# Cosine attention and highway FFN on one core: batch 0 by query tiles, k on seven-token lanes, batch 0's norms by Ln and Exp

## The chip, the core and the metric

The kernel runs on one core of a Trainium2 chip. The core has five instruction queues: PE (TensorE, matmuls and their weight loads), DVE (VectorE), ACT (ScalarE), POOL (GpSimd) and SP (SyncE, which here only issues DMAs). The time is the device time of one execution in microseconds; less is better. Inputs and output lie in HBM, the on-chip memories are SBUF (128 lanes, here also called partitions) and PSUM (eight banks of 128 x 512 fp32), into which PE writes.

## What is computed

q, k and v are 8 batches x 12 heads x 448 tokens x 64 fp32. Rows of q and k are divided by their norms, so the scores are cosines over tau = 0.1. After a softmax over keys and the product with v, the heads of a token stand side by side (768 wide) and go through a highway layer.

```python
q_n = q / (np.linalg.norm(q, axis=-1, keepdims=True) + 1e-06)
k_n = k / (np.linalg.norm(k, axis=-1, keepdims=True) + 1e-06)
attn = softmax(q_n @ k_n.T / tau)          # per batch and head
x = (attn @ v) as [8 * 448, 12 * 64]
H = np.maximum(x @ w_h, 0.0)
T = sigmoid(x @ w_t + b_t)
out = T * H + (1.0 - T) * x
```

Since the cosines are at most 1, the kernel leaves out the subtraction of the maximum: exp(10) is harmless. It computes in fp16 with fp32 sums.

## The kernel before

**Layout.** The 12 heads of a batch make 6 pairs (head p and p + 6) and 3 groups of 2 pairs. q is loaded so that a lane holds seven neighbouring tokens ("seven-token lanes": 64 lanes for the even heads, 64 for the odd ones, 1792 contiguous bytes each). k and v are loaded otherwise: 384 tokens as 128 lanes of three tokens, and the last 64 tokens by a DMA of their own (`kt`, `vt`). q comes by SP's queue as fp32; k and v by POOL's queue, which casts to fp16 on the way. For batch 0 alone k comes as fp32 in six pieces by ACT's and SP's queues, into the output buffers `os` (`ld_k0`).

**Stages of a batch.** Squares on ACT (L368, L388 and L391, tails L402), sums of squares on DVE (L376, L397, L404), the inverse root on DVE by a bit trick and two Newton steps, seven small instructions (`newton`, L416 to L423; four times for batch 0, on parts), scaling to fp16 on POOL (q L434, k L495, tails of k L502; a few on DVE in batch 0), transposes on PE through PSUM (q L446, k L460 and L465) and copies back to SBUF on DVE (L451, L471; in pieces L473, L475 for batch 0).

For each pair then: six score matmuls of 448 queries, in twos that use the two halves of the array (`scores`, L531), one for the tail keys of both heads (L542), seven exps of 448 columns on ACT (L537, L544), and `attend`: per 128 queries one product with the tail of v (L556) and six with v (L561), for the last queries eight half-wide ones (L569). The column of ones in `vp` gives the sum of the softmax; DVE takes its reciprocal (L576) and evicts the product into `x` (L577). `vp` is filled by copies on DVE (L509) and, for the tail, casts on POOL (L519).

`ffn` works on 128 tokens at a time, three such tiles and a half one per batch: transposes of x on PE (L600), a copy (L602), products with w_t and then w_h (L616, in the half tile L613), the bias on DVE (L625), tanh on ACT (L632; the sigmoid is 0.5 tanh(z/2) + 0.5), gate arithmetic on DVE (L628, L634, L637), the last addition on POOL (L642; at the end DVE), the store on SP (L652, L649). All four tiles of a batch read `x` as one piece, so none starts before all six pairs of that batch are attended.

**Order.** Nothing is scheduled by the compiler. All operations of all batches are made as a list (`op`, class `Plan`), with the tiles they read and write. `ORDER` is a permutation of that list, written out as numbers, and `SLOTS` says which buffer of each ring every tile takes. Each engine executes its operations in this order, one after the other. So batches overlap as ORDER has it: loads, norms and transposes of later batches stand between scores of one and FFN tiles of another. The main loop also adds waits of its own ("port"): a POOL operation of certain kinds waits for the DVE operation of such a kind that stands before it. Before any real work PE executes 18 matmuls on zeros (L279).

Of the kernel before, what the change touches and what calls it, by code (L numbers as in the profile page):

```python
# [8 lines left out]
FP32 = mybir.dt.float32  # L9
# [120 lines left out]
}  # L130


PORT = ("nt", "gt", "gg", "vc", "qn", "kn", "kb", "vt", "out")


class Op:
# [65 lines left out]
def kernel(  # L202
# [11 lines left out]
    nc = tc.nc  # L214
# [555 lines left out]
```

## Time and profile before

| what | us |
|---|---|
| median of 3 runs | 271.3 (270.35 to 271.45) |
| the profiled execution | 270.06 |
| its span, first to last instruction | 268.3 |
| PE busy | 251.6 |
| DVE busy | 233.4 |
| ACT busy | 214.5 |
| POOL busy | 169.8 |
| mean granted PE clock | 0.958 of full |

The span is the time between the first and the last instruction in the profile; the execution's own time is somewhat longer. A matmul's end is modelled, so a PE that is busy throughout is not thereby at its best. In the rows that follow, L12 is line 12 of the kernel, "B" are PSUM banks, and "<-" in a wait names what ended it.

### The profile page before, as it was taken

To read this page: it belongs to the slowest core of one execution; us is meant where nothing else is said; L and a number is where in the kernel's file an instruction comes from. 1 tells how busy PE (TensorE), PEld (TensorE's weight loads), DVE (VectorE), ACT (ScalarE), POOL (GpSimd) and SP (SyncE) were. 2 spreads that over 40 slices of the span, in tenths; PEclk is the share of its full clock that TensorE was granted. 3 is DMA by queue.
4 is the path that set the end of the run, shared out by engine and by line. 5 is a ranking of instruction groups with operands and counts; after the bars stand their busy time and mean duration, and the time that the engine had idled before them with its cause. 6 is when DMAs were issued, how large, how long until landed. Compare 5 with 4: busy or idle time off the path is not lost.

```text
span 268.3 us, 7687 instructions
## 1 busy us (share of the span) xinstructions
PE 251.6 (94%) x3042; PEld 158.8 (59%) x3042; DVE 233.4 (87%) x523; ACT 214.5 (80%) x421; POOL 169.8 (63%) x212
## 2 busy tenths in 40 slices
PE   8375999999999999999999999999999999999990
PEld 2122566656756576657656685666666675667660
DVE  2987988799999999999989899999998788657993
ACT  3389899999589997999899996999979757883120
POOL 6467878306975679668957397659555686320650
PEclk9755799999999999999999999999999999999998
DMA  7999999999307990496995972990513101052146
GB/s 173 298 290 181 208 270 261 213 255 126 44 18 221 234 182 14 146 257 159 151 142 185 164 107 67 330 135 4 147 23 100 29 15 49 0 147 65 29 135 190
DMA packets 51092, 38.64 MB, mean 144 GB/s; under 512 B 37488, under 2 KB 47856, under 8 KB 51056
## 3 DMA queue, kind: packets, MB, share of 16 engines
q1 hardware_dynamic: 25888, 26.75, 36.2%
q0 software_dynamic: 24896, 11.21, 33.1%
q8 instruction: 24, 0.39, 0.5%
q10 hardware_dynamic: 272, 0.20, 0.2%
q14 instruction: 12, 0.10, 0.1%
HBM read 38.34 MB, written 11.01 MB: 184 GB/s over the span
## 4 chain that ended last, share of the span: by engine, by line
PE 81%; DMA 6%; DVE 4%; ACT 4%; SPq 1%; issue 1%; POOL 1%; ACTq 0%; DVEq 0%
PE B L616 33%; PE B L531 12%; PE B L561 10%; PE B L613 5%; DMA os<-in_k_dram 4%; PE B L556 4%; PE B L600 4%; PE B L446 3%; PE B L542 3%; PE B L569 3%; PE B L460 3%; ACT E L537 3%; DMA out_dram<-os 1%; PE B L465 1%; DVE hm L628 1%
## 5 line engine op out<-in xcount | busy, mean ns | idle before, releaser
L537 ACT ACTIVATE E<-B 128x448 f16<-128x448 f32 x288 | 137.4, 577 | 15.6 <-PE B L531 12.6
L642 POOL TENSOR_TENSOR os<-x,hm 128x384 f32<-128x384 f16 x53 | 47.5, 911 | 50.2 <-DVE hm L637 39.6
L616 PEld LDWEIGHTS <-xT 128*128 128x128 f16 x576 | 51.2, 98 | 34.8 <-issue 7.5
L434 POOL TENSOR_TENSOR qn<-qr,y 128x448 f16<-128x448 f32 x47 | 43.4, 934 | 24.6 <-issue 8.1
L616 PE MATMUL B<-wh,xT 128*128 128x384 f16 x288 | 57.6, 326 | 0.0
L616 PE MATMUL B<-wt,xT 128*128 128x384 f16 x288 | 56.7, 326 | 0.0
L531 PE MATMUL B<-qT,kT 64*128 64x448 f16 x288 | 43.5, 367 | 2.8 <-DVE kT L473 1.5
L561 PE MATMUL B<-vp,E 128*128 128x65 f16 x864 | 44.5, 195 | 0.0
L561 PEld LDWEIGHTS <-E 128*128 128x128 f16 x864 | 39.1, 99 | 2.9
L632 ACT ACTIVATE tt<-z 128x768 f16<-128x768 f32 (+1 forms) x32 | 25.3, 793 | 18.5 <-DVE z L625 14.8
L495 POOL TENSOR_TENSOR kp<-kr,y 128x384 f16<-128x384 f16 x42 | 34.3, 827 | 8.2 <-DVE tt L634 2.6
L628 DVE SCALAR_TENSOR_TENSOR hm<-B,x 128x384 f16<-128x384 f32 x56 | 30.5, 549 | 3.0 <-PE B L616 1.7
L556 PE MATMUL B<-vp,Et 128*128 128x130 f16 x144 | 32.3, 224 | 0.0
L625 DVE TENSOR_TENSOR z<-B,bias 128x384 f32<-128x384 f32 x48 | 25.9, 551 | 6.5 <-PE B L616 5.5
L544 ACT ACTIVATE Et<-B 128x448 f16<-128x448 f32 x48 | 27.9, 597 | 3.1 <-PE B L542 2.8
L577 DVE SCALAR_TENSOR_TENSOR x<-B,rd 128x448 f16<-128x448 f32 x48 | 29.2, 617 | 0.6
L376 DVE TENSOR_REDUCE n<-sq 128x14 f32<-128x896 f32 (+1 forms) x25 | 25.8, 1040 | 1.2 <-ACT sq L368 1.2
L397 DVE TENSOR_REDUCE n<-sq 128x18 f32<-128x1152 f32 (+2 forms) x17 | 21.5, 1269 | 4.2 <-ACT sq L388 3.8
L368 ACT ACTIVATE sq<-qr 128x896 f32<-128x896 f32 (+1 forms) x24 | 23.1, 978 | 1.1 <-DMA qr<-in_q_dram 1.1
L531 PEld LDWEIGHTS <-kT 64*128 64x128 f16 x288 | 10.3, 94 | 20.1 <-issue 12.3
L556 PEld LDWEIGHTS <-Et 128*128 128x128 f16 x144 | 14.1, 98 | 7.9 <-issue 4.7
L542 PE MATMUL B<-qT,kT 128*128 128x448 f16 x48 | 17.4, 371 | 1.1 <-DVE kT L475 1.1
(59 smaller groups left out, 363.3 us busy)
## 6 DMA issues: line engine op xcount, KB each, us to landing
qr<-in_q_dram SPq DMA_DIRECT2D x7, 1344.0 KB, 7.6
out_dram<-os SPq DMA_DIRECT2D x48, 192.0 KB, 3.3
kr<-in_k_dram POOLq DMA_DIRECT2D x7, 576.0 KB, 12.2
vr<-in_v_dram POOLq DMA_DIRECT2D x7, 576.0 KB, 10.3
kt<-in_k_dram SPq DMA_DIRECT2D x16, 96.0 KB, 6.4
vt<-in_v_dram SPq DMA_DIRECT2D x16, 96.0 KB, 7.5
out_dram<-os SPq DMA_DIRECT2D x16, 96.0 KB, 2.9
qr<-in_q_dram SPq DMA_DIRECT2D x3, 448.0 KB, 6.9
```

Of the source, the lines that this page charges most:

```text
L434: ENG[eng].tensor_mul(R("qn", 3 * b + g)[:, :, t, :], R("qr", b)[:, g + 3 * t, :].rearrange("l (j d) -> l j d", d=D), R("y", b)[:, c : c + ...
L495: ENG[eng].tensor_mul(R("kp", 6 * b + p).rearrange("l c t d -> l t c d"), a, kcol(b, p))
L531: nc.tensor.matmul(R("B", ("S", n, c, t))[:, 0:S], lhsT=R("kT", i)[ln, s, 128 * c : 128 * c + 128], rhs=R("qT", i)[ln, s, :], start=True, ...
L537: nc.scalar.activation(R("E", n)[:, at : at + 7, :].rearrange("l j x -> l (j x)"), R("B", ("S", n, c, t))[:, 0:S], AF.Exp)
L544: op("ACT", f"expt {n}", lambda: nc.scalar.activation(R("Et", n).rearrange("l j x -> l (j x)"), R("B", ("St", n))[:, 0:S], AF.Exp), r=[("B ...
L556: nc.tensor.matmul(U[:, 2 * c : 2 * c + 2, :], lhsT=Et[:, 2 * c : 2 * c + 2, :].rearrange("l j x -> l (j x)"), rhs=vp[:, 6:8, 0:65], start ...
L561: nc.tensor.matmul(U[:, 2 * c + t, :], lhsT=E[:, at : at + 2, :].rearrange("l j x -> l (j x)"), rhs=vp[:, 3 * t + m, 0:65], start=False, s ...
L577: op("DVE", f"ev {n}", lambda: nc.vector.scalar_tensor_tensor(out=R("x", b)[:, :, D * p : D * p + D], in0=U_()[:, :, 0:D], scalar=0.0, in1 ...
L616: nc.tensor.matmul(P[:, 0:MH], lhsT=xT[:, cc, :], rhs=w_[:, cc, MH * mh : MH * mh + MH], start=(cc == 0), stop=(cc == CC - 1))
L625: op("DVE", f"za {g} {mh}", lambda at=at, sl=sl: nc.vector.tensor_add(R("z", g)[:, sl], R("B", at)[:, 0:MH], biast[:, :] if tail else bias ...
L628: op("DVE", f"hm {g} {mh}", lambda at=at, sl=sl, mh=mh: nc.vector.scalar_tensor_tensor(out=R("hm", g)[:, sl], in0=R("B", at)[:, 0:MH], sca ...
L642: op(eng, f"out {g} {mh}", lambda sl=sl, mh=mh: ENG[eng].tensor_add(R("os", g)[:, sl], xpart(mh), R("hm", g)[:, sl]), r=[("gg", g), ("x", ...
```

## The change

**k like q.** k is loaded on seven-token lanes by one DMA per batch (three for batch 0, one per group), always on POOL's queue with the cast. One function now does each stage for q and k: `ld_qk`, `norm`, `scale`, `turn`. A group of k takes seven transposes instead of eight; the DMA for the tail, its square, its sum, its two multiplies (L502) and the buffers `kt`, `kb`, `kp` are gone. The last 64 keys of both heads of a pair still need a block-diagonal tile for the tail scores, so the copy to SBUF is now one of 2 x 384 columns and two of 64 lanes x 2 x 64 columns (`cpt`), into buffers whose other halves were set to zero at the start. v follows the same assignment of tokens: it comes by two DMAs of 64 lanes, its tail is each lane's seventh token.

**Batch 0 by query tiles.** `attend0` takes a group and a tile of 128 queries (the fourth: 64), with scores of 128 (64) columns, exps of 512 and 384 columns, and its own eviction. The FFN's tiles of batch 0 read only the matching part of x, so `ffn(0, i)` can stand as soon as the three groups are attended for tile i. Group 0's turned q and k lie in a spare slot of the ring `x`.

**Norms of batch 0.** y = exp(-0.5 ln(n2 + 1e-14)) by two ACT operations per group in place of Newton. Ln is in another table set of ACT than tanh, so set 6 is loaded at the start and set 0 after the third of these (`table2`).

**Order and rings.** `ORDER` and `SLOTS` are new throughout ("searched for two cases" in the words of the change). Rings: qT and kT 4 deep instead of 3, xT 5 instead of 3, kn 3. The loads of later q and of the tails of v on SP (`held`) now wait for the ACT operation that stands before them in ORDER. There is also code for turning x by DMA, which is off (`XDMA = ()`).

Where the pieces stand now: on POOL the first k load is the first instruction, the other two follow the constants, then v, k of batch 1 and w_t; w_h stands behind the first two scalings of batch 1's k. On ACT 33 exps stand ahead of PE's first FFN matmul (59 before). On PE the first FFN matmul has 296 matmuls ahead of it (341 before), warm-up included.

```diff
-PORT = ("nt", "gt", "gg", "vc", "qn", "kn", "kb", "vt", "out")
+PORT = ("nt", "gt", "gg", "vc", "qn", "kn", "vt", "out")
...
+        self.held = eng == "SP" and kind in ("ldq", "ldvt") and name.split()[1] != "0"
...
+    GROUPS = ((0, 1), (1, 2), (2, 3)), ((0, 1), (1, 3)), ((0, 3),)
+    LG = ((0, 0), (0, 28), (0, 56))
...
+    op("ACT", "table", lambda: table(6), w=[("t6",)])
...
+    def ld_qk(nm, b, gs=range(3)):
+        t, eng = (q, "SP") if nm == "q" else (k, "POOL")
+
         def fn():
-            d, a = R("qr", b), q_src(b)
+            d, a = R(nm + "r", b), q_src(t, b)
             if len(gs) == 3:
                 ENG[eng].dma_start(d[:, :, :], a)
             else:
                 ENG[eng].dma_start(d[:, gs[0] :: 3, :], a[:, :, gs[0] :: 3, :])
...
+    def lnexp(b, lo, hi, parts):
+        i = (b, lo)
+        op("ACT", f"ln{hi - lo} {b} {lo}", lambda: nc.scalar.activation(
+            R("tu", i)[:, 0, lo:hi], R("n2", b)[:, lo:hi], AF.Ln, bias=eps[:, 0:1]),
+           r=[("n2", b) + p for p in parts] + [("eps",), ("t6",)], w=[("nt", i)], u=[("tu", i), ("n2", b)])
+        op("ACT", f"ie{hi - lo} {b} {lo}", lambda: nc.scalar.activation(
+            R("y", b)[:, lo:hi], R("tu", i)[:, 0, lo:hi], AF.Exp, scale=-0.5),
+           r=[("nt", i)], w=[("y", b) + p for p in parts] + [("lg", i)], u=[("tu", i), ("y", b)])
...
+        if nm == "k":
+            for t in range(2):
+                ln = slice(64 * t, 64 * t + 64)
+                op("DVE", f"cpt {b} {g} {t}", lambda ln=ln, t=t: nc.vector.tensor_copy(
+                    turned("k", i)[ln, :, 384 + 64 * t : 448 + 64 * t], src()[ln, :, 384:448]),
...
+    def attend0(g, i):
+        q_, k_ = turned_of(g)
+        w = 128 if i < 3 else 64
...
+            def fq(ss=ss, A=A, B_=B_, o=o):
+                for s in ss:
+                    for c in range(NC):
+                        for t in range(2):
+                            ln, at = slice(64 * t, 64 * t + 64), unit(s)[0][t][c] - o - 512 * t
+                            nc.tensor.matmul(R("B", (A, B_)[t])[:, at : at + w], lhsT=k_()[ln, s, 128 * c : 128 * c + 128],
+                                             rhs=q_()[ln, s, 128 * i : 128 * i + w], start=True, stop=True)
...
+            for t, X, m in ((0, A, 512), (1, B_, 384)):
+                op("ACT", f"ex{m} {n}", lambda X=X, m=m, t=t, o=o: nc.scalar.activation(
+                    flat()[:, o + 512 * t : o + 512 * t + m], R("B", X)[:, 0:m], AF.Exp),
...
     def ffn(b, i):
         g = 4 * b + i
+        xk = ("x", b) if b else ("x", b, i)
...
+    op("ACT", "table2", lambda: table(0), r=[("lg", i) for i in LG], w=[("t0",)])
...
+        if b == 0:
+            for i in range(4):
+                for g in range(NG):
+                    attend0(g, i)
...
+                if o.eng == "ACT":
+                    act = made[-1]
+                elif o.held:
+
+                    behind(made[0], act)
```

More of the change, by code (lines that the diff above doesn't have):

```diff
@@ L144, in __init__ @@
         kind = name.split()[0].rstrip("0123456789")
-        self.port = eng in ("DVE", "POOL") and (kind in PORT or kind == "sqq")
+        self.held = eng == "SP" and kind in ("ldq", "ldvt") and name.split()[1] != "0"
+        self.port = eng in ("DVE", "POOL") and (kind in PORT or kind == "sq")
 class Plan:
@@ L221 @@
     WARM = 18
+    XDMA = ()
+    GROUPS = ((0, 1), (1, 2), (2, 3)), ((0, 1), (1, 3)), ((0, 3),)
+    LG = ((0, 0), (0, 28), (0, 56))
+    SCALE = {("q", 0, 0): ("DVE", "POOL"), ("k", 0, 0): ("DVE", "POOL")}
     tau = float(tau)
@@ L267, in zero, with table @@
         return fn
-    op("ACT", "table", lambda: nc.scalar.activation(tab[:1, :], nc.const_aps.tensor(0.0, [1, 1]), AF.Exp), w=[("tab",)])
+    def table(n):
+        return nc.scalar.add_instruction(mybir.InstLoadActFuncSet(
+            name=nc.get_next_instruction_name(), engine=nc.scalar.engine, act_func_set_id=n))
+    op("ACT", "table", lambda: table(6), w=[("t6",)])
     op("POOL", "ident", lambda: make_identity(nc, ident), w=[("id",)])
@@ L344, in ld_b, with col @@
         op("SP", "ldb", fn, w=[("b",)])
[L347 to L366 removed]
+    def col(nm, g):
+        return 28 * g + 14 * (nm == "k")
@@ new lines, with norm, fn @@
+    SQV = ()
+    SPLIT = {("q", 0, 0): ("ACT", "DVE"), ("k", 0, 0): ("ACT", "ACT")}
+    def norm(nm, b, g):
+        i = (nm, b, g)
+        sc = tau if nm == "q" else 1.0
+        engs = SPLIT.get(i, (("DVE" if i in SQV else "ACT"),))
+        n = 3 - len(engs)
+        for t, eng in enumerate(engs):
+            ts = slice(t, t + n)
+            def fn(eng=eng, ts=ts):
+                src = R(nm + "r", b)[:, g::3, :][:, ts]
+                dst = R("sq", i).rearrange("l (t x) -> l t x", t=2)[:, ts]
@@ L448, in turn_q, with src @@
+        def src():
+            return R16(at)[:, 0:896].rearrange("p (s x) -> p s x", s=2)
         for s in range(2) if parts == 2 else (None,):
             def cp(s=s):
-                a = slice(0, 896) if s is None else slice(448 * s, 448 * s + 448)
-                nc.vector.tensor_copy(R("qT", i).rearrange("p s x -> p (s x)")[:, a], R16(("Tq", i))[:, a])
-            op("DVE", f"cpq{parts} {b} {g} {s}", cp, r=[("B", ("Tq", i))], w=[("qT", i, s)] if s is not None else [("qT", i, 0), ("qT", i, 1)])
@@ L700 @@
-        scale_kb(b, "POOL")
-        if b == 0:
-            copy_v(b, 0, 3)
-            copy_v(b, 3, 6)
-        else:
-            copy_v(b, 0, 6)
+            if b == 0:
+                ld_w(moe_w_t, wt, "wt")
+                ld_w(moe_w_h, wh, "wh")
+                ld_b()
+        else:
+            ld_qk("q", b)
+            ld_qk("k", b)
+            ld_v(b)
+            ld_vt(b)
+        for g in range(NG):
+            for nm in "qk":
+                norm(nm, b, g)
+        for g0, g1 in GROUPS[min(b, 2)]:
+            (lnexp if (b, 28 * g0) in LG else newton)(b, 28 * g0, 28 * g1, [(nm, g) for g in range(g0, g1) for nm in "qk"])
@@ L706 @@
+        for p0 in (0, 3) if b == 0 else (0,):
+            copy_v(b, p0, p0 + (3 if b == 0 else 6))
         cast_vt(b, "POOL")
         for g in range(NG):
-            first = b == 0 and g == 0
-            scale_q(b, g, ("DVE", "POOL") if first else ("POOL", "POOL"))
-            for s in range(2):
-                scale_k(b, 2 * g + s, "DVE" if first else "POOL")
-            turn_q(b, g, 2 if first else 1)
-            turn_k(b, g)
-        for p in range(NP):
-            scores(b, p)
-            attend(b, p)
+            for nm in "qk":
+                scale(nm, b, g, SCALE.get((nm, b, g), ("POOL", "POOL")))
+                turn(nm, b, g, 1)
@@ L717, with behind @@
+        if b == 0:
+            for i in range(4):
+                for g in range(NG):
+                    attend0(g, i)
+        else:
+            for p in range(NP):
+                scores(b, p)
+                attend(b, p)
         for i in range(4):
             ffn(b, i)
+    def behind(a, b):
+        tc.add_manual_dep(a, b.name, mybir.DependencyInfo(mybir.DependencyClass.Sync, mybir.DependencyReason.SCHED_ONLY),
+                          reason="order")
     with nc.allow_low_precision(reason="fp16 operands of the products and gates as given"):
@@ L721 @@
         with tc.manual_schedule():
-            before = None
+            before = act = None
             for o in pl.ordered(ORDER, SLOTS):
@@ L725 @@
                 o.fn()
-                if o.port:
-                    made = [i for i in nc.cur_bb.bb.instructions[made:] if i.engine == ENG[o.eng].engine]
-                    if o.eng == "DVE":
-                        before = made[-1]
-                    elif before is not None:
-                        tc.add_manual_dep(made[0], before.name, mybir.DependencyInfo(
-                            mybir.DependencyClass.Sync, mybir.DependencyReason.SCHED_ONLY), reason="port")
-                        before = None
+                made = [i for i in nc.cur_bb.bb.instructions[made:] if i.engine == ENG[o.eng].engine]
+                if o.eng == "ACT":
+                    act = made[-1]
+                elif o.held:
+                    behind(made[0], act)
+                elif o.port and o.eng == "DVE":
+                    before = made[-1]
+                elif o.port and before is not None:
+                    behind(made[0], before)
+                    before = None
 _INS = ['q', 'k', 'v', 'tau', 'moe_w_h', 'moe_w_t', 'moe_b_t']
```

378 lines of the change are left out of this document (163 added, 215 removed), and 147 rows, old and new, of the table ORDER.

## The prediction

> **What bounds the kernel now.** I read the page first: busy time by engine and the rows by slices.
>
> ```profile
> PE 251.6 (94%) x3042; PEld 158.8 (59%) x3042; DVE 233.4 (87%) x523; ACT 214.5 (80%) x421; POOL 169.8 (63%) x212
> ...
> PE   8375999999999999999999999999999999999990
> ...
> PEclk9755799999999999999999999999999999999998
> DMA  7999999999307990496995972990513101052146
> ```
>
> TensorE is full from the fifth slice to the last but one. What is not full is the start: four slices in which PE is 30 to 80% busy, partly at half clock, while the DMA row stands at 9 up to 67 us. The split into stages gives the numbers (columns: stretch, its length, then busy us and instruction count of PE, its weight loads, DVE, ACT, POOL, then granted clock, DMA share, GB/s).
>
> ```profile
> 12.00:30.00 18.00, 13.26 (x85) 6.24 (x86) 15.04 (x41) 14.54 (x27) 14.42 (x19) 0.50 1.32 232
> ...
> 60.00:200.00 140.00, 139.87 (x1797) 91.02 (x1797) 134.08 (x284) 126.90 (x246) 102.75 (x122) 1.00 0.69 136
> 200.00:258.00 58.00, 58.00 (x730) 38.45 (x729) 46.04 (x105) 37.38 (x77) 29.15 (x36) 1.00 0.21 53
> 258.00:268.30 10.30, 4.07 (x37) 2.25 (x34) 6.06 (x14) 1.37 (x2) 1.74 (x2) 0.90 0.73 210
> ```
>
> From 60 to 200 us PE sets the pace, and DVE has only 5.9 us of 140 to spare. From 12 to 30 us PE issues 85 matmuls in 18 us, against 12.8 per us later, at a granted clock of 0.50. So there are two questions: how soon does the changed start get PE onto steady work, and does the middle still fit on DVE. The chain of waits and the timeline place the start.
>
> ```profile
> 16.86 2.80 ACT E L537 x7
> ...
> 43.93 1.00 PE B L600 x18
> ```
> ```profile
> 1.26 1.28 ACT L388 ACT_TABLE_LOAD   x1 [1.26 <-PEq L751]
> ...
> 6.00 0.56 ACT L368 ACTIVATE sq<-qr 128x448 f32<-128x448 f32 x1
> ...
> 11.34 0.62 DVE L434 TENSOR_TENSOR qn<-qr,y 128x448 f16<-128x448 f32 x1
> ...
> 16.77 4.43 ACT L537 ACTIVATE E<-B 128x448 f16<-128x448 f32 x10
> ...
> 28.06 0.29 PE L556 MATMUL B<-vp,Et 128*128 128x130 f16 x1
> ...
> 45.79 2.12 PE L616 MATMUL B<-wt,xT 128*128 128x384 f16 x12
> ```
>
> The exps begin at 16.8 us, the products with v at 28.1, the first matmul of the FFN at 45.8. The FFN of batch 0 needs all six pairs of heads with all their queries, which the change undoes.
>
> **The change, part by part.** *PE's work.* Prices at full clock, from the chain:
>
> ```profile
> 101.69 0.39 PE B L446 x7
> ...
> 103.39 0.67 PE B L531 x6
> ...
> 105.14 0.19 PE B L542
> ...
> 108.90 0.06 PE B L556
> 108.96 0.19 PE B L561 x6
> ...
> 110.56 0.24 PE B L569 x7
> ```
> ```profile
> 56.50 2.44 PE B L616 x15
> ...
> 68.97 1.95 PE B L613 x24
> ```
>
> A transpose costs 0.056 us (0.39/7), a score matmul 0.112, a tail score 0.19, a 128-query product with v 0.25, a tail product about 0.25, an FFN matmul 0.163, one of the half-wide tail 0.081. A batch is 66 transposes (3.7), 36 scores (4.0), 6 tail scores (1.1), 18 products (4.5), 6 tails (1.5), 72 + 24 FFN matmuls (11.7 + 1.9): 28.4 us, and eight are 227.5. Ahead of its first FFN matmul the old order issues 93 transposes, 48 scores, 8 tail scores, 18 products, 6 tails: 5.2 + 5.4 + 1.5 + 4.5 + 1.5 = 18.1 us, so 209.4 are left at 45.8. PE really ends near 262.1 (4.07 busy us after 258.0): 216.3 us for 209.4, a factor of 1.033.
>
> The new order issues ahead of its first FFN matmul 61 transposes (3.4), 102 of batch 0's 144 small scores and 17 of 24 small tail scores (about 0.71 of 5.1, so 3.6), and 14 products (3.5): 10.5 us. In all k needs 7 transposes a group, not 8: 24 fewer, 1.3 us. So 226.2 - 10.5 = 215.7 are left, 6.3 more than before, or 6.5 at the factor. The new kernel breaks even if that first matmul starts at 45.8 - 6.5 = 39.3 us. The small scores (128 and 64 columns, each with its own weights) are not in this trace. Below, their price is that of the wide ones by column, 5.1 us for the batch; above, a transpose's 0.056 for each 128 columns with no pair running together, about 8.3. Only the 0.28 still to come counts here: 0 to 0.9 us. I take 0.1, since the wide scores do run in pairs (0.112 each against 0.19 for a lone one of the same width).
>
> *When that matmul starts.* The first k now comes through POOL's queue. Nearest rows:
>
> ```profile
> wt<-in_moe_w_t_dram POOLq DMA_DIRECT2D x1, 1152.0 KB, 20.3
> wh<-in_moe_w_h_dram POOLq DMA_DIRECT2D x1, 1152.0 KB, 24.3
> ...
> vr<-in_v_dram POOLq DMA_DIRECT2D x4, 144.0 KB, 9.8
> ...
> os<-in_k_dram ACTq DMA_DIRECT2D x1, 192.0 KB, 4.8
> ```
> ```profile
> DMA to landing us min/median/max: 6.0/12.8/19.4
> ```
>
> The old first k took 4.8 us on ACT's queue; v's loads on POOL's took 6.0 at best (the second fence) and 9.8 in the middle. k is now POOL's first DMA, with only q beside it, so I take 6.0: landed at 6.8 us, and 10.5 as the late end. Then, in the order in which ACT and DVE now stand:
>
> ```profile
> L537 ACT ACTIVATE E<-B 128x448 f16<-128x448 f32 x288 | 137.4, 577 | 15.6 <-PE B L531 12.6 <-PE B L561 1.1 <-PE B L569 0.7
> ...
> L434 POOL TENSOR_TENSOR qn<-qr,y 128x448 f16<-128x448 f32 x47 | 43.4, 934 | 24.6 <-issue 8.1 <-DVE tt L634 4.5 <-DVE y L423 4.0
> ...
> L376 DVE TENSOR_REDUCE n<-sq 128x14 f32<-128x896 f32 x23 | 24.7, 1077 | 1.2 <-ACT sq L368 1.2
> L368 ACT ACTIVATE sq<-qr 128x896 f32<-128x896 f32 x23 | 22.5, 996 | 1.1 <-DMA qr<-in_q_dram 1.1
> L471 DVE COPY kT<-B 128x1024 f16<-128x1024 f16 x21 | 14.3, 681 | 0.7 <-PE B L465 0.7
> ...
> L502 POOL TENSOR_TENSOR kb<-kt,y 64x384 f16<-64x384 f32 x16 | 13.6, 852 | 3.0 <-DVE y L423 1.8 <-DVE vp L509 0.6
> ...
> L602 DVE COPY xT<-B 128x768 f16<-128x768 f16 x24 | 12.8, 549 | 0.7 <-PE B L600 0.7
> ...
> L519 POOL CAST vp<-vt 64x384 f16<-64x384 f32 x16 | 8.0, 500 | 3.1 <-PE B L616 2.6
> ...
> L475 DVE COPY kT<-B 128x256 f16<-128x256 f16 x3 | 0.8, 283 | 0.0
> ```
>
> Two squares of k at 0.56 (7.9), the square of the second q that stands before Ln (8.9), Ln and Exp at about 0.25 each, somewhat under a 448-wide exp's 0.48 (137.4/288) (9.4), then on DVE one reduction of 1.08 and two scalings of 0.6 (11.7), seven transposes of k at half clock, 0.8 (12.5), two more reductions that stand ahead of the copies (by 13.9), four copies, 1.6 (15.5), and a score: first exp at about 16.0, late end 19.7. From there ACT issues 33 exps (15.7 at 0.48), two squares (2.0), one Ln and one Exp (0.5) and the second table load (1.28 by the row above) before the first FFN matmul: 19.5 us, so 35.5 if ACT never waits. In the old start it was busy 14.54 of 18 us; at that share it would be 40. I take 36.5, nearer the full case: batch 0's Newton chains (four of seven DVE instructions) are gone, and what ACT waited for there, the norms of the later groups, comes out of ACT itself. 39.3 - 36.5 leaves 2.8 us, less the 0.1 above: **2.7 us faster**.
>
> On that table load ACT is the engine that sets the pace, so it counts in full. The Trainium skill (ScalarE: Activation LUTs, What ACT_TABLE_LOAD costs) gives 1.28 us for a load, as the row has it, and about 1.38 more for a drain at every switch of set. No row here shows the drain, the only load standing at the start; by the page the sum would be 1.3 us instead of 2.7 faster.
>
> *DVE.* k's copy shrinks from 1024 to 768 columns (0.681 to 0.549, row L602), but two copies of 128 columns by 64 lanes join it. The nearest row is 256 columns, 0.283; at the slope to 768 (0.52 per 1000) that is 0.22 each. So +0.29 a group; 15 groups lie in 60 to 200 us: 4.4 us into 5.9 free. Lower end 0, upper end 4.4 lost. I cost it at nothing: the cover is that idle time, and 12 us after 200 into which the new order can shift. Batch 0's evictions become 9 + 3 pairs instead of 6, about +1.5 us in the start, where the Newton steps that leave return about as much or more.
>
> *POOL and queues.* The 16 tail multiplies of k leave (13.6 us), the others grow from 384 to 448 columns, and v comes as two DMAs per batch; POOL is idle for 98 of 268 us, so nothing. On SP k's 16 tail loads leave. The loads of later q and v tails now wait for ACT, and stores queue behind them: there are four output buffers to hold them, so nothing; uncovered, POOL's last add would wait, then the FFN. Tail of the program: same operations, nothing.
>
> The profiled execution took 270.06 us, 1.24 below the median. 270.06 - 2.7 = 267.4, and beside the median 271.3 - 2.7 = **268.6 us**.
>
> **Rivals.** (A) *DVE becomes the bound in the middle, slower.* At 134.1 of 140 us it may hold no more, as the idle rest is made of short waits for matmuls. Then 4.4 (15 groups) to 6.1 us (21) are lost: 273.0 to 274.7. It decides from 2.7 us on. For: the stage row. Against: PE alone has no idle there, and DVE's share falls to 46.0 of 58 after 200.
> (B) *wh arrives late, slower.* Its DMA stands on POOL behind batch 1's first scalings, about 33.8 us (first exp 16.0, 16 exps, the load, a square, a reduction, Newton, two scalings), 10 us later than now.
>
> ```profile
> L335 POOL DMA_DIRECT2D wt<-in_moe_w_t_dram x1: 884/884/884, 17.3 to 17.3; - x1
> L335 POOL DMA_DIRECT2D wh<-in_moe_w_h_dram x1: 882/882/882, 23.2 to 23.2; - x1
> ```
>
> Between the landings of wt (17.3 + 20.3) and wh (23.2 + 24.3) lie 9.9 us, so wh lands at 43.7 at best; the matmul that needs it stands some 8 us of PE work behind the first FFN one, at 44.5. 4 us late gives 272.6; up to 0.8 is free.
> (C) *The start is no earlier: the change does not do what it is built for.* k lands near 10.5, or ACT drains at the switch and waits as it did: 39 us, 271.1.
> (D) *More.* PE's 10.5 us ahead of the FFN take 21 at a clock of 0.50, from 12 to 33 us, close to what ACT needs; so at half clock each hinders the other. If the clock rises by 20 us, with products running from about 21 instead of 28 (norms of the second group near 14.5, then six scalings of 0.93 and two casts of 0.50 on POOL), ACT alone counts: 34.4, 266.5. The Trainium skill (TensorE: Matmul & The Clock Gate, Part 1) has the clock rise after some 3.4 us of sustained matmuls, which would speak for (D); here PE was 74% busy for 18 us and stayed at 0.50, so scattered work did not do it.
>
> **How the numbers follow.** Forecast 0.38, own range 267.0 to 269.9; D 0.17; C 0.18; A 0.15; B 0.12. A measurement of this kernel can tell about 0.5% from no change, 269.9 to 272.7. Faster 0.55 (forecast, D), same 0.18 (C), slower 0.27 (A, B). The range goes from 264.5 (D with an exp at 15) to 273.6, most of A.
>
> **What would show it.** Right: first exp near 16, first product with v near 21, first FFN matmul near 36.5 us, PE full after it. Wrong: that matmul after 39; DVE over 98% busy from 60 to 200 with PE waiting on copies; a wait for wh's DMA between 40 and 50 us; more than 1.3 us without ACT work at the second table load.

## The result and the profile after

The changed kernel takes 271.92 us (median of 16 runs, 270.55 to 273.91), the kernel before on the same chip 270.50. The ratio is 1.0053 with a 95% interval of 1.0030 to 1.0077: slower by half a per cent, where 1% faster was forecast. The profiled execution took 271.84 us. From here on times are medians of runs beside the kernel before, whose own median in these groups of runs was 269.84 to 270.46. So a difference in us between two experiments carries up to 0.6 us of that, and where it matters the difference of the ratios, taken at 270 us, is given beside it.

The page of the changed kernel, busy time by engine and the rows by slices:

```profile
PE 249.3 (92%) x3144; PEld 160.1 (59%) x3144; DVE 232.2 (86%) x554; ACT 217.7 (81%) x425; POOL 166.1 (62%) x205
...
PE   7188897999999999999999999999999999999991
...
PEclk9855999999999999999999999999999999999998
DMA  7998289799959990795709740993043002304265
```

The start is denser: PE's third to sixth slices went from 7, 5, 9, 9 to 8, 8, 8, 9, and the half clock ends sooner. But the seventh slice, 40 to 47 us, has a 7, and the last has a 1 instead of a 0. By stages (stretch, length, busy us and count of PE, weight loads, DVE, ACT, POOL, then clock, DMA share, GB/s):

```profile
12.00:30.00 18.00, 13.53 (x174) 9.62 (x175) 13.53 (x30) 14.63 (x30) 10.03 (x12) 0.62 0.92 161
30.00:44.00 14.00, 13.14 (x244) 9.42 (x240) 12.41 (x41) 13.72 (x29) 6.84 (x8) 1.00 0.84 166
44.00:60.00 16.00, 14.04 (x170) 8.82 (x171) 12.17 (x30) 13.87 (x30) 11.45 (x14) 1.00 1.00 191
60.00:200.00 140.00, 138.73 (x1769) 88.46 (x1770) 135.34 (x311) 128.92 (x250) 97.74 (x116) 1.00 0.72 151
...
258.00:270.00 12.00, 6.02 (x51) 3.50 (x48) 7.49 (x17) 2.21 (x3) 2.70 (x4) 0.92 0.56 138
```

From 12 to 30 us the clock is 0.62 instead of 0.50. From 44 to 60 PE is idle for 2 us, where the kernel before had none, and ACT is idle as long. From 60 to 200 DVE has 4.7 us idle left. The timeline places the steps, ScalarE first, then PE:

```profile
17.48 0.95 ACT L371 ACTIVATE sq<-qr 128x896 f32<-128x896 f32 x1 [2.91 <-DMA qr<-in_q_dram]
18.34 0.47 ACT L568 ACTIVATE E<-B 128x384 f16<-128x384 f32 x1
...
19.41 1.08 ACT L568 ACTIVATE E<-B 128x512 f16<-128x512 f32 x2
20.51 1.28 ACT L285 ACT_TABLE_LOAD   x1
21.80 2.73 ACT L568 ACTIVATE E<-B 128x384 f16<-128x384 f32 x6
```
```profile
24.69 0.29 PE L579 MATMUL B<-vp,E 128*128 128x130 f16 x1
...
25.22 0.54 PE L582 MATMUL B<-vp,E 128*128 128x65 f16 x6
...
26.11 0.35 PE L582 MATMUL B<-vp,E 128*128 128x65 f16 x6
...
34.93 1.62 PE L662 MATMUL B<-wt,xT 128*128 128x384 f16 x9
```

The first exp is at 18.3 us, the first product with v at 24.7, the first matmul of the FFN at 34.9, 10.9 us sooner than before. By the prediction's break-even at 39.3 us that alone would be 4.4 us faster: 270.06 - 4.4 = 265.7. The profiled execution took 6.1 us more than that. One wait is plain, from the list of waits between 40 and 60 us (total, times, longest) and from the rows of w_h's tile:

```profile
PE B L662 <- DMA wh<-in_moe_w_h_dram: 1.4, 1, 1.4
```
```profile
L340 POOL DMA_DIRECT2D wh<-in_moe_w_h_dram x1: 895/895/895, 33.9 to 33.9; - x1
...
DMA to landing us min/median/max: 11.3/11.3/11.3
```

w_h's load is issued at 33.9 and lands at 45.2.

Where PE's lead went can be followed in the work that it still has to do: all matmuls that start after a given time, each counted once, times the prediction's unit prices (the small scores by column; us of work; later kernels beside it):

```
left at us        44     60     80    100    200    258
before         211.8  196.7  177.2  157.7   61.0    3.7
after          207.9  194.8  177.6  159.2   62.6    5.7
both edits     206.9  192.4  175.1  156.4   60.0    3.1
and masked     206.4  191.8  174.2  154.9   57.3    0.0
```

The changed kernel is 3.9 us ahead at 44, 1.9 at 60, and behind from 80 on; at 258 it is 2.0 behind, and its profiled execution took 1.8 us longer.

### The profile page after: what moved, and what is told of

It reads as the page before. It is cut to its first block, busy times and chain, and to the rows that moved or that the text cites. A ratio compares the mean times of both kernels' runs of the same rounds, so it can differ in the third digit from the quotient of the medians.

```text
span 269.9 us, 7912 instructions
## 1 busy us (share of the span) xinstructions
PE 249.3 (92%) x3144; PEld 160.1 (59%) x3144; DVE 232.2 (86%) x554; ACT 217.7 (81%) x425; POOL 166.1 (62%) x205
## 3 DMA queue, kind: packets, MB, share of 16 engines
q0 software_dynamic: 20416, 12.58, 33.9%
## 4 chain that ended last, share of the span: by engine, by line
PE 54%; DVE 5%; ACT 1%; issue 1%; POOL 0%; DVEq 0%
PE B L662 25%; PE B L478 7%; PE B L508 6%; PE B L433 4%; PE B L659 3%; PE B L638 2%; PE B L489 2%; PE B L503 2%; PE B L516 2%; DVE hm L674 1%; DVE x L524 1%; ACT E L484 1%; DVE z L671 1%; DVE hm L683 1%; ACT tt L678 0%
## 5 line engine op out<-in xcount | busy, mean ns | idle before, releaser
L484 ACT ACTIVATE E<-B 128x448 f16<-128x448 f32 x252 | 119.7, 567 | 17.4 <-PE B L478 15.5
L688 POOL TENSOR_TENSOR os<-x,hm 128x384 f32<-128x384 f16 x53 | 47.7, 916 | 36.5 <-DVE hm L683 10.6
L418 POOL TENSOR_TENSOR kn<-kr,y 128x448 f16<-128x448 f16 x47 | 43.5, 937 | 32.6 <-DVE y L397 10.2
L379 DVE TENSOR_REDUCE n<-sq 128x14 f32<-128x896 f32 (+1 forms) x50 | 50.7, 1036 | 2.9 <-ACT sq L371 2.9
L508 PE MATMUL B<-vp,E 128*128 128x65 f16 x756 | 38.3, 193 | 0.0
L478 PE MATMUL B<-qT,kT 64*128 64x448 f16 x252 | 35.8, 354 | 0.1
L508 PEld LDWEIGHTS <-E 128*128 128x128 f16 x756 | 33.6, 98 | 3.5 <-issue 1.0
L674 DVE SCALAR_TENSOR_TENSOR hm<-B,x 128x384 f16<-128x384 f32 x56 | 30.4, 547 | 5.3 <-PE B L662 4.7
L371 ACT ACTIVATE sq<-kr 128x896 f32<-128x896 f16 (+1 forms) x25 | 23.6, 967 | 3.0 <-DMA kr<-in_k_dram 3.0
L524 DVE SCALAR_TENSOR_TENSOR x<-B,rd 128x448 f16<-128x448 f32 x42 | 25.2, 615 | 0.5
L568 ACT ACTIVATE E<-B 128x384 f16<-128x384 f32 (+1 forms) x42 | 20.0, 629 | 0.7 <-PE B L582 0.4
L433 PE MATMUL B<-ident,qn 128*128 128x128 f16 x168 | 14.1, 227 | 6.5 <-POOL qn L418 5.9
L648 DVE COPY xT<-B 128x768 f16<-128x768 f16 (+1 forms) x32 | 15.7, 501 | 2.6 <-PE B L638 1.6
```

The costliest lines, as they stand in the source:

```text
L371: nc.scalar.activation(dst, src, AF.Square, scale=sc)
L379: nc.vector.reduce_sum(R("n2", b)[:, c : c + 7 * n], a, axis=AX.X)
L418: ENG[eng].tensor_mul(R(nm + "n", i)[:, :, t, :], R(nm + "r", b)[:, g + 3 * t, :].rearrange("l (j d) -> l j d", d=D), R("y", b)[:, c : c + ...
L478: nc.tensor.matmul(R("B", ("S", n, c, t))[:, 0:S], lhsT=R("kT", i)[ln, s, 128 * c : 128 * c + 128], rhs=R("qT", i)[ln, s, :], start=True, ...
L484: nc.scalar.activation(R("E", n)[:, at : at + 7, :].rearrange("l j x -> l (j x)"), R("B", ("S", n, c, t))[:, 0:S], AF.Exp)
L508: nc.tensor.matmul(U[:, 2 * c + t, :], lhsT=E[:, at : at + 2, :].rearrange("l j x -> l (j x)"), rhs=vp[:, 3 * t + m, 0:65], start=False, s ...
```

## Experiments

**Is it w_h?** Two kernels move only the place of w_h's load in the written order (38 is that load): early, behind w_t's, or later, behind loads of batches 1 and 2.

```diff
+ORDER = moved(ORDER, 38, 37)     # early: right behind the load of w_t
+ORDER = moved(ORDER, 38, 542)    # the other kernel: behind k of batch 2
```

> The changed kernel with one DMA issue moved: w_h's load stands right behind w_t's on POOL (issued near 10 us instead of 34). Theory W (w_h came too late: PE waited 1.4 us for it at 44 us, ACT and DVE stood still behind PE and could not make it up later because they are nearly full): no wait for w_h, PE's work done by 60 us up from 34.4 to 36 us or more, by 100 us from 70.5 to 73 or more, time 2 to 5 us under the changed kernel, that is 0.987 to 0.998 of the kernel before. Rival D (DVE, with two more copies per group of k, is the bound from 60 to 100 us): the wait at 44 us goes, but by 100 us PE is no further on than 71.5, and the time moves by under 1 us (1.002 to 1.006).

> The changed kernel with w_h's load moved the other way, behind the loads of batch 1's v and batch 2's k on POOL (issued near 39 us). W: each us that w_h lands later costs a us or more; with a landing some 6 us later (51 us) the time rises by 5 to 8 us, 1.022 to 1.035 of the kernel before. D: DVE works off its queue during the wait and catches up, so the time rises by less than half of the delay, under 3 us, below 1.017.

Early: 269.70 us, ratio 0.9983 (0.9960 to 1.0007); later: 281.36, ratio 1.0412 (1.0375 to 1.0448). The stretch of the early one, then the later one's wait:

```profile
44.00:60.00 16.00, 15.97 (x191) 9.81 (x190) 14.37 (x34) 15.78 (x32) 11.57 (x14) 1.00 0.65 155
```
```profile
PE B L670 <- DMA wh<-in_moe_w_h_dram: 9.8, 1, 9.8
```

Early, PE is full from 44 to 60. Later, w_h lands at 52.9, PE waits 9.8 us, 8.4 more than in the changed kernel, and the time grows by 9.4, more than was expected: what PE waits there is lost at least one for one. So the late w_h costs the changed kernel about 2.2 us (271.92 - 269.70; 1.9 by the ratios), and the other 4 us are elsewhere.

**Are the held loads to blame?** The later loads of q and of v's tails wait, by a rule of the new order, for ScalarE. Without it:

```diff
-                elif o.held:
-                    behind(made[0], act)
```

> The changed kernel without the rule that later loads of q and v's tails on SP wait for ACT's place in the order (the loads wait for their buffers only). In the changed kernel ACT waited 2.9 us at 14.6 us for q of batch 1, a load that this rule held back to 11 us, and the first exp came at 18.3. If that wait is what the start costs: first exp near 16.5, first FFN matmul near 33, and 1 to 2 us less in all (0.998 to 1.002). W and D both expect that the gain is eaten at w_h, which then waits longer: within 1 us of the changed kernel (1.002 to 1.009).

269.39 us, ratio 0.9972 (0.9947 to 0.9996). This is 2.5 us under the changed kernel, where at most 1 was expected. The wait of 2.9 us for q goes, the first exp is 1.4 us sooner and the first FFN matmul 0.85 (34.08):

```profile
16.98 0.49 ACT L568 ACTIVATE E<-B 128x384 f16<-128x384 f32 x1 [0.69 <-PE B L555]
```

No wait for w_h shows here: it was issued at 33.1 and took 8.9 us to land. So this edit and the first remove the same loss. Both at once:

> Both edits at once: the load of w_h moved up behind that of w_t, and the later loads of q and of v's tails free to start without a wait for ScalarE. Nothing of the computation changes. Alone the first gave 269.7 us (ratio to the kernel before 0.9983), the second 269.39 us (0.9972), the changed kernel 271.92. In both PE was 3.8 to 5.2 us ahead of the kernel before at 44 us and had lost most of it by 100 us. Theory N (from 60 to 100 us VectorE and ScalarE are packed with the norms of batches 2 and 3, and PE waits there): the two edits don't add up, since either one already removes the wait for w_h and what remains is lost in that stretch: 269.0 to 269.6 us, PE's lead at 100 us under 2 us. Rival S (the two losses are separate and add up): 2.2 + 2.5 us off 271.9, 267.2 us, ratio 0.990.

269.04 us, ratio 0.9955 (0.9937 to 0.9973): they hardly add up, as the first theory said. 3.6 us stay (first FFN matmul at 34.75, so 265.5 by the break-even; the profiled execution took 269.07). Its stages:

```profile
44.00:60.00 16.00, 15.96 (x203) 10.07 (x202) 14.37 (x32) 15.82 (x32) 13.23 (x17) 1.00 0.45 114
60.00:200.00 140.00, 138.74 (x1759) 88.51 (x1756) 135.35 (x312) 128.77 (x251) 96.94 (x114) 1.00 0.70 143
```

**Are DVE or ACT packed with norms from 60 to 100 us?** My first theory for the rest, since PE's lead shrinks there while DVE does 14 reductions. Three kernels without the held loads leave out batch 2's reductions, batch 2's squares, or batch 6's reductions; a fourth, with both edits, leaves out squares and reductions of batches 2 and 3.

```diff
-            op("DVE", f"rd{n} {nm} {b} {g} {t}", fr, ...
+            op("DVE", f"rd{n} {nm} {b} {g} {t}", fr if b != 2 else (lambda: None), ...
```

> The kernel without the held loads (269.39 us alone) and without the six reductions on VectorE that sum the squares of batch 2's q and k (6 of 1.07 us, at 55 to 63 us); batch 2's norms are then those of batch 0. The squares on ScalarE stay. Theory N, VectorE: these reductions stand in one lump ahead of the FFN's evictions and PE waits for those, so 2 to 3 us are gained, 266.5 to 267.4 us, and PE's work done between 60 and 80 us rises from 17.6 to about 19.5 us. Rival X (ScalarE is what is full there: 10.00 of 10 us busy from 30 to 40, 40 to 50 and 60 to 70): under 0.8 us, 268.6 to 269.4 us. Rival A (VectorE is the bound throughout): 5 to 6.4 us, 263 to 264.4 us.

> The kernel without the held loads and without the six squares on ScalarE of batch 2's q and k (6 of about 1 us, at 54 to 61 us); their reductions on VectorE stay and sum the squares that an earlier batch left in the buffers. Theory N, VectorE: ScalarE only had to be in step with VectorE, so under 1 us is gained, 268.4 to 269.4 us. Rival X (ScalarE is what is full there): 2 to 3 us are gained, 266.5 to 267.4 us. If both engines hold PE up in turn, each of the two kernels gains 1 to 2 us.

> The kernel without the held loads and without the six reductions of batch 6 (some 6.4 us of VectorE between 165 and 215 us); batch 6's norms are then those of batch 4. It takes as much work from VectorE as the kernel without batch 2's reductions, in a stretch where the kernel of before and the changed one advance alike. Theory N: the loss is in the place, so under 0.8 us are gained, 268.6 to 269.4 us. Rival A (VectorE is the bound throughout): 4 to 6 us, 263.4 to 265.4 us, as much as for batch 2.

> The kernel with both edits (w_h early and no held loads, 269.04 us) without the norms of batches 2 and 3: 12 squares on ScalarE (about 12 us) and 12 reductions on VectorE (12.9 us) are left out, nearly all of them between 54 and 100 us; those two batches take the norms of batches 0 and 1. Leaving out one batch's reductions, or its squares, gained 0.5 and 0.1 us. Theory N2 (VectorE and ScalarE hold PE up in turn, so that either alone hides behind the other): 2.5 to 4 us gained, 265.0 to 266.5, and the time that PE's matmuls take beyond their unit prices between 60 and 80 us falls from 2.6 us to under 1. Theory P (the loss lies in PE's own order of work: more changes between kinds of matmul that use all, half the rows or half the columns, 0.07 us each in every stretch of the traces, and short waits on results asked for as soon as they can be there): under 1 us gained, 268.0 to 269.0, and the excess stays over 2 us.

They took 268.82, 269.28 and 268.98 us against 269.39, and 267.18 against 269.04. The theory falls for either engine alone: 6.4 us of DVE gone from one place bring 0.6 us, from another 0.4, 6 us of ACT 0.1, and none of the three is clear of the noise (ratios 0.9953, 0.9965 and 0.9974 against 0.9972, each uncertain by 0.002). 25 us of both bring 1.9, between the two forecasts, and PE does only 0.4 us more work from 60 to 80 us than with both edits. The work did go, as two stretches show, first without the held loads, then without batch 2's reductions as well:

```profile
50.00:60.00 10.00, 10.00 (x133) 6.54 (x132) 9.29 (x20) 9.82 (x19) 8.82 (x12) 1.00 0.53 155
60.00:70.00 10.00, 9.46 (x153) 6.26 (x150) 9.75 (x28) 10.00 (x20) 4.89 (x6) 1.00 1.32 209
```
```profile
50.00:60.00 10.00, 9.94 (x133) 6.45 (x132) 6.48 (x17) 9.95 (x19) 9.00 (x12) 1.00 0.56 159
60.00:70.00 10.00, 9.52 (x153) 6.43 (x153) 7.25 (x23) 10.00 (x19) 4.88 (x6) 1.00 1.33 210
```

DVE is 5.3 us less busy and PE issues the same matmuls.

**Ln and Exp undone.** Batch 0's inverse roots by Newton again, in the kernel with both edits, without the second table load:

```diff
-        op("ACT", f"ln{hi - lo} {b} {lo}", ...activation(..., AF.Ln, ...))
-        op("ACT", f"ie{hi - lo} {b} {lo}", ...activation(..., AF.Exp, scale=-0.5))
+        op("DVE", f"ln{hi - lo} {b} {lo}", steps, ...)      # the seven instructions of newton
+        op("DVE", f"ie{hi - lo} {b} {lo}", lambda: None, ...)
```

> The kernel with both edits (269.04 us) with one part of the change undone: batch 0's reciprocal norms by Newton on VectorE (three times seven instructions of some 0.2 us, 4.4 us) in place of Ln and Exp on ScalarE (three times two) and without the second table load of 1.28 us. Theory T (ScalarE sets the pace up to the FFN, so what it doesn't do counts): first exp 0.5 to 1 us later, but ScalarE is relieved of 2.8 us before the first FFN matmul, which comes up to 1.5 us sooner; 267.8 to 269.0. Rival (the chain to the first exp counts, VectorE stands in it): first exp 1 us later, the second and third group's norms later as well, 269.5 to 271.

271.92 us, ratio 1.0069 (1.0048 to 1.0091): 2.9 slower than with both edits (3.1 by the ratios), more than the rival's 271. First exp and first FFN matmul of this kernel:

```profile
19.99 0.87 ACT L585 ACTIVATE E<-B 128x384 f16<-128x384 f32 x2 [1.43 <-PE B L572]
```
```profile
37.68 1.62 PE L679 MATMUL B<-wt,xT 128*128 128x384 f16 x9
```

The first exp is 2.4 us later, the first FFN matmul 2.9 and so is the end, so the rival holds: the chain to the first exp counts. It also shows again that the FFN's start is worth its microseconds.

**The small copies of k's tail.** A kernel with the changed order leaves them out for batches 1 to 7 (zeros in their place), a second does so with both edits:

```diff
-                op("DVE", f"cpt {b} {g} {t}", lambda ln=ln, t=t: nc.vector.tensor_copy(
+                op("DVE", f"cpt {b} {g} {t}", lambda ln=ln, t=t: None if b else nc.vector.tensor_copy(
```

> The changed kernel without the two small copies of k's last 64 keys, for batches 1 to 7 (42 DVE instructions of 0.23 us, 9.7 us of DVE in all, some 6.5 of it between 60 and 200 us); the scores of those keys are then of zeros. D: PE is fed from 60 to 100 us, time 3 us or more under the changed kernel (0.994 of the kernel before or less). W: the 5.5 us that PE lost between 44 and 100 us mostly stay, time within 1.5 us of the changed kernel (1.000 to 1.007).

> The kernel with both edits (269.04 us) without the two small copies of k's tail per group of batches 1 to 7 (42 of 0.217 us, 9.1 us of VectorE); those batches' scores of the tail keys come from zeros. In the changed kernel that took 271.92 to 269.63 us though the wait for w_h stood. Theory D (VectorE's added work is lost everywhere): 266.5 to 267.3. Rival (it helped to make up for the wait for w_h, which the two edits remove): 268.4 to 269.2.

269.63 us (ratio 0.9997, 0.9968 to 1.0026) against 271.92, and 266.24 (0.9867, 0.9843 to 0.9891) against 269.04: 2.3 and 2.8 us (1.5 and 2.4 by the ratios). So 9.1 us of copies are worth several times what 6.4 us of reductions are. DVE's timeline of the changed kernel shows what is different about them:

```profile
80.79 0.45 DVE L456 COPY vp<-vr 128x1152 f16<-128x1152 f16 x1
81.15 0.21 DVE L449 COPY kT<-B 64x128 f16<-64x128 f16 x1
81.29 1.00 DVE L671 TENSOR_TENSOR z<-B,bias 128x384 f32<-128x384 f32 x2
82.32 0.23 DVE L449 COPY kT<-B 64x128 f16<-64x128 f16 x1
82.58 1.09 DVE L379 TENSOR_REDUCE n<-sq 128x14 f32<-128x896 f32 x1
83.70 0.56 DVE L443 COPY kT<-B 128x768 f16<-128x768 f16 x1
```

The first copy starts 0.08 us before the instruction ahead ends, and the next starts 0.07 before its own end; of the 372 pairs of other neighbours that wait for nothing 359 overlap so too, by 0.08 us in the median. The second starts 0.03 after the end ahead, the next 0.03 after its own end, and even the one behind that, the next to read PSUM, waits out the reduction. Of the 48 small copies 20 are overlapped by the next instruction, 25 are followed by a gap of up to 0.06 us and three by a longer wait. A copy of the first kind takes 0.13 us from its start to the next (median), one of the second 0.26, and this one also starts 0.11 us later than it would with an overlap: 0.37 in all. The Trainium skill (VectorE: DVE Perf Modes, Two Vector instructions with no wait between them) has this as a rule: an instruction is held until all earlier ones are done where its input or output starts in another group of 32 lanes than the last one in that memory. By that rule the copy on lanes 64 to 127 is the held one. Two kernels tell it apart by leaving out one of the two:

> The kernel with both edits (269.04 us) without the small copy of k's tail on lanes 0 to 63 of batches 1 to 7 (21 of 0.217 us); the tail scores of those heads come from zeros there. Leaving out both copies gave 266.24. In the traces the small copies fall into two kinds of equal number: one overlaps its neighbours on VectorE by 0.08 us like all other instructions, the other starts 0.03 us after the end of the one ahead and the next starts 0.03 us after its own end. By start to start the first costs 0.14 us, the second 0.36. Theory H (the second kind is the copy on lanes 64 to 127, which can't overlap): leaving out the lower one takes 2.9 us from VectorE of 10.5, so 0.8 of the 2.8 us: 268.0 to 268.5. Rival E (both cost the same): 1.4 us, 267.3 to 267.9.

> The same without the small copy on lanes 64 to 127 (21). Theory H: it takes 7.6 us from VectorE, 2.0 of the 2.8 us: 266.8 to 267.3, and no small copy of batches 1 to 7 is left with a gap instead of an overlap. Rival E: 1.4 us, 267.3 to 267.9, and half of those left still show the gap.

Without the lower copy 267.81 us (ratio 0.9919, 0.9889 to 0.9949), without the upper 266.01 (0.9848, 0.9818 to 0.9877): 1.2 and 3.0 us below 269.04 (1.0 and 2.9 by the ratios), for instructions of nearly equal length (0.21 and 0.23 us). The first time lies in the rival's range, 267.3 to 267.9, the second below both ranges, and the two together are more than the 2.8 us of leaving out both. But the rival asked for equal times, and they differ by 1.8 us, with intervals that don't meet. The same place in the kernel that keeps the upper copies, then in the one that keeps the lower ones:

```profile
77.79 1.01 DVE L679 TENSOR_TENSOR z<-B,bias 128x384 f32<-128x384 f32 x2
78.83 0.23 DVE L457 COPY kT<-B 64x128 f16<-64x128 f16 x1
79.09 1.09 DVE L387 TENSOR_REDUCE n<-sq 128x14 f32<-128x896 f32 x1
```
```profile
77.64 0.44 DVE L464 COPY vp<-vr 128x1152 f16<-128x1152 f16 x1
78.00 0.21 DVE L457 COPY kT<-B 64x128 f16<-64x128 f16 x1
78.14 1.00 DVE L679 TENSOR_TENSOR z<-B,bias 128x384 f32<-128x384 f32 x2
```

In the kernel with the upper copies a small copy is followed by such a gap 23 times and by an overlap once, in the one with the lower copies by an overlap 19 times and by a gap five times (batch 0 keeps both kinds in either). The trace agrees with the rule.

**Kernels that keep the work.** One gives the tail to GpSimd (DVE copies 896 columns, GpSimd moves the upper lanes' part and clears its place); one writes the tail twice through a mask, on all 128 lanes:

```diff
+                nc.vector.tensor_mul(turned("k", i)[:, :, 384:512].rearrange("p s (h x) -> p s h x", h=2),
+                                     src()[:, :, 384:448].unsqueeze(2).to_broadcast([128, 2, 2, 64]),
+                                     mask[:, :, :].unsqueeze(1).to_broadcast([128, 2, 2, 64]))
```

> Computes all. The kernel with both edits (269.04 us), with k's tail of batches 1 to 7 put in place by GpSimd instead of VectorE: VectorE's copy of k takes 896 columns instead of 768 (0.615 against 0.547 us) and the two copies of 0.217 us go, so 0.37 us less for each of 21 groups, 7.7 us in all; GpSimd copies 64 lanes by 128 columns and clears the place they came from, at an estimated 0.2 to 0.4 us each, in its queue behind the scalings. Theory D: 267.0 to 268.0. Rival: the tail scores wait for GpSimd's queue, 269.5 to 271. If VectorE's copies cost nothing: 268.7 to 269.4.

> Computes all. The kernel with both edits (269.04 us) with the two small copies of k's tail, in all groups but the first, replaced by one multiplication on VectorE over all 128 lanes: 256 columns, the tail twice, by a mask of ones and zeros. The nearest row for its duration is the 128x256 eviction of the attention, 0.418 us; with the usual overlap that is 0.34 us from start to start against 0.14 + 0.36 for the two copies, so 3.7 us less VectorE time in 23 groups. Theory H (time on VectorE counts, at 2.8 us for 10.5): 1.0 us, 268.0. If the copy that can't overlap costs more than its time (leaving it out alone gained 3.0 us): down to 266.8. Rival (one long instruction in place of two short ones gains nothing): 268.7 to 269.4.

On GpSimd 267.87 us (ratio 0.9933, 0.9910 to 0.9956); its two operations took 336 and 236 ns. With the mask 265.89 (0.9838, 0.9791 to 0.9885), the best of all and below the lowest forecast, 266.8: 1.6% faster than the kernel before. Its DVE:

```profile
69.40 0.55 DVE L453 COPY kT<-B 128x768 f16<-128x768 f16 x1
69.87 0.28 DVE L458 TENSOR_TENSOR kT<-B,mask 128x256 f16<-128x256 f16 x1
70.07 0.55 DVE L665 COPY xT<-B 128x768 f16<-128x768 f16 x1
```
```profile
60.00:200.00 140.00, 139.40 (x1777) 89.25 (x1774) 134.59 (x306) 129.15 (x253) 97.21 (x113) 1.00 0.70 142
```

Twice the columns take 0.20 us from start to start, where the pair took 0.13 + 0.37. From 60 to 200 us DVE is almost as busy as with the copies, 134.59 against 135.35, and PE does 134.6 us of work instead of 132.4. Lastly the mask alone, without the other two edits:

> Computes all. The changed kernel (271.92 us) with the one multiplication by a mask in place of the two small copies as the only edit; w_h stays late and the loads stay held. With both of those edits the same replacement took 269.04 to 265.89 us. Theory H+W (the copy on the upper lanes and the late w_h are two separate losses of about 3 us each): 268.5 to 269.2, and PE still waits 1 to 3 us for w_h. Rival (the two hide one another): 270 to 271 us, or under 267.5 if the wait for w_h goes with it.

270.28 us, ratio 1.0001 (0.9967 to 1.0035), with runs from 268.50 to 272.16. That is 1.6 us below the changed kernel but above the 269.2 of the theory, in the range that the rival gave. The profiled execution, the slowest of the twelve, shows that the other loss grew:

```profile
PE B L671 <- DMA wh<-in_moe_w_h_dram: 3.9, 1, 3.9
...
47.32 3.80 PE L671 MATMUL B<-wh,xT 128*128 128x384 f16 x12 [3.91 <-DMA wh<-in_moe_w_h_dram]
...
47.40:50.90 3.50, 3.50 (x12) 1.70 (x13) 0.58 (x2) 0.00 (x0) 0.00 (x0) 0.51 1.24 191
```

w_h took 13.4 us to land there, 11.3 in the changed kernel's profile: the late load costs another amount in each execution. And the wait costs more than its length: behind it the granted clock is 0.51 for 3.5 us, and twelve matmuls take 3.6 us, 2.0 by price. A stretch at half clock also goes with the waits for w_h of 2.9 us (in the first kernel without the small copies, 45.5 to 48.8 us) and of 9.8 us (w_h later, 46.9 to 57.0), but not with the 1.4 us of the changed kernel's trace. From 60 to 200 us PE did 134.1 us of work here against 132.2, so the mask's gain in the middle is the 2 us that it is with both edits. Whether the longer wait belongs to this kernel or to the executions that were profiled is not settled; the two slowest of the twelve runs, 272.09 and 272.16, have the lowest mean granted clocks, 0.957 and 0.960 against 0.966 to 0.970.

## Why the prediction was wrong

**When the FFN starts, and what that is worth: right, the time in part by luck.** Forecast 36.5, measured 34.9. That a microsecond of this start is a microsecond of the end is borne out twice, by the wait of 9.8 us and by Newton. On the way some sizes were off, and they cancelled. k landed at 7.8 us instead of 6.8 and ACT waited 2.9 us for a held q, so the first exp came at 18.3 instead of 16.0; the first product at 24.7 instead of 21. From the first exp to the first FFN matmul 20.5 us were allowed, ACT's 19.5 and one of waiting, and it took 16.6: 31 exps stood there, at 0.43 us from start to start where they followed one another, not 33 at 0.48, and ACT was idle for 0.4 us.

**The table load: right.** 1.28 us; the exp behind it starts at 21.80, where the load ends. The further 1.38 us that the Trainium skill (ScalarE: Activation LUTs, What ACT_TABLE_LOAD costs) gives for a drain are not seen.

**"I cost it at nothing" (DVE): the step that failed most.** The copies' duration was right, 0.22 us forecast and 0.217 measured. Their price was not in the duration: the upper one takes 0.37 us of DVE's stream, since neither it nor what follows overlaps, and the idle 5.9 us of DVE were no cover. The mask shows 3.1 us (269.04 - 265.89; 3.2 by the ratios). Rival A had the place and, with 4.4 us, roughly the size; its reason, DVE full, was not the reason, since leaving out reductions gained little.

**w_h: a rival at 0.12 that came true.** It landed at 45.2, not 43.7, and was wanted at 43.9, not 44.5. It costs 2.2 us by the early load, 2.9 with both edits. The steps that the prediction names for the issue at 33.8 add up to about 30.4 (7.7 for 16 exps, 1.3, 1.0, 1.1, seven Newton instructions of about 0.2, 1.9 for two scalings, all behind 16.0), so that it was issued at 33.9 is in part luck. I had it as one case among others, though nothing excluded that it and A hold at once. With either taken away the time is near the kernel before (ratios 0.9983 and 1.0001); with both it is slower.

**The sum.** With both losses away the first FFN matmul is at 34.47 us; 39.3 - 34.5 = 4.8 us faster gives 265.2 for the profiled execution, which took 265.9. The break-even rule therefore holds to 0.7 us. In the changed kernel itself the 4.4 us of the start less 2.9 for w_h and 3.1 for the copies leave 1.6 us lost, and its profiled execution lost 1.8. The time lies near rival C's 271.1 by chance: C had the start no earlier, and it was 10.9 us earlier.

**Clock and rest.** Rival D asked for full clock by 20 us. In the trace a product's six matmuls take 0.54 us at 25.2 and 0.35 at 26.1, and PE has no idle between 22.1 and then: some 3.6 us of steady work. The Trainium skill (TensorE: Matmul & The Clock Gate, Part 1) says about 3.4. In the other traces it took from 3.0 us to 6.4 (without the upper copies) behind PE's last idle time, so the 3.6 of one trace confirms no figure. In three of them (reductions of batch 2, norms of batches 2 and 3, or both small copies left out) full clock came at 19.5 to 19.8 us, as D asked, but was lost again within 3.5 us. In the changed kernel's trace D's condition failed, and the FFN still started only 0.5 us behind D's 34.4.

What stays open is part of the stretch from 60 to 80 us. In these 20 us PE does 17.2 us of work by price in the changed kernel and 19.5 before. A matmul behind which the next works on another part of the array (the whole, half its rows, L478, or half its columns, L659) takes 0.10 us more than its price there, in the median of either trace, and the new order has 20 such changes there instead of 11:

```profile
66.81 0.36 PE L478 MATMUL B<-qT,kT 64*128 64x448 f16 x2
67.10 0.68 PE L659 MATMUL B<-wh,xT 128*64 128x384 f16 x6
67.71 0.36 PE L478 MATMUL B<-qT,kT 64*128 64x448 f16 x2
```

Two score matmuls take 0.29 us there, against 0.224 by price. Nine more changes are some 0.9 us and PE is idle for another 0.5, together less than the 2.3 that it falls behind; no order with fewer changes was tried. Open too is why upper copies, 21 of 0.37 us, are worth 3.0 us and 6.4 us of reductions 0.6 at most: no run moved the one to the place of the other.

## What to carry to other kernels

Price a small instruction by what starts behind it, not by its duration: look for a gap where its neighbours overlap, above all where it works on other lanes than they do. An engine's idle share is no cover for work that its stream must pass in order, and two rivals that exclude each other in no way should be added up, not weighed one against the other. When work moves earlier, list every transfer that it needs by its new time, the one behind a moved instruction in the same queue first.

## What the hardware showed that was not expected

- A copy of 64 x 128 on lanes 64 to 127 costs DVE 0.37 us, 0.26 from its start to the next and 0.11 by its own late start; the same copy on lanes 0 to 63 costs 0.13, and a multiplication of twice its columns on all lanes 0.20.
- Leaving out 25 us of squares and reductions on two nearly full engines gained 1.9 us; leaving out 21 upper copies of 0.23 us gained 3.0.
- The landing time of one load of 1152 KB on POOL's queue lay between 8.9 and 31.6 us, by its place among the other loads and by the execution (11.3 and 13.4 in the same place).
- PE's waits of 2.9, 3.9 and 9.8 us in the middle of the kernel went with 3.4 us or more at half clock, a wait of 1.4 us did not.
